# Fifteen trains of unread TensorE passes behind the last store of a fused convolution and feed-forward kernel

## The chip, the cores and the metric

The kernel runs on one core of a Trainium2 chip (trn2). The metric is the time of one execution on the device in microseconds, the median of several runs; lower is better.

## The reference

Two steps follow each other. A dynamic convolution over the sequence takes a softmax over seven taps for each token and head and sums seven shifted copies of the input with these weights; its result, 32768 tokens of 192 numbers, goes through two matrix products with a squared ReLU between them (2048 hidden units).

```python
w = np.exp(weight_gen - max); w = w / (w.sum(-1) + 1e-9)     # 8 x 4096 x 8 heads x 7 taps
x_unf = x_pad[:, idx, :].reshape(B, S, K, H, group)          # seven shifted copies of x
x = np.einsum('bshk,bskhg->bshg', w, x_unf).reshape(B * S, 192)
r = np.maximum(x @ w_in, 0.0)                                # w_in 192 x 2048
out = (r * r) @ w_out                                        # w_out 2048 x 192
```

## The kernel before

The 32768 tokens are laid over 128 partitions, 256 tokens each, and go through in 64 chunks of four tokens per partition (512 tokens, `N`). For every chunk VectorE makes the softmax and the tap sums, the result is turned so that the 192 features lie on partitions, and TensorE then does the first product (`mm1`, line 430) and the second (`mm2_turned`, line 503). The precision of a float32 product is kept with passes over two parts: a rounded high part and the remainder (`xh`, `xl` of the input; `gh`, `gl` of the squared ReLU; two parts of each weight in `W` and `V`), all of type float32r. A pass has a 64-row or 128-row weight (`LDWEIGHTS`) and a moving operand of up to 512 columns. The passes of 64 rows come in pairs, for the upper and the lower half of the array's rows, and the two halves of a pair write two banks of PSUM.

ScalarE makes ReLU, square and `gh` (lines 447, 451, 455), VectorE makes `gl` (line 459). The order of the work is written out by hand: the program is issued in the order of the code, and lists of functions (`todo`, `soon`, `late`, `pend`) say behind which pair of hidden blocks a piece of another chunk stands. The first chunk's second product is a float32 one (line 467), with the weights still unsplit.

The last chunk is done another way. Its ReLU writes the tokens in another order (lines 443, 445), and its second product runs with the activations as weights and `V` as the moving operand (line 476, 384 and 192 columns in turn). Behind it `finish` and `store` put out the four tokens one by one: four passes of line 767 and eight of line 770, VectorE's last sum (line 773) and the last store (line 774, issued in line 557). The pools with rotating buffers that the change draws on are `ps_h` (four PSUM banks, tag `ph`), `gp` (eight buffers each of `rg`, `gh`, `gl`) and `att` (`xT`).

Of the kernel before, what the change touches and what calls it, by code (L numbers as in the profile page):

```python
# [8 lines left out]
F32 = mybir.dt.float32  # L9
F32R = mybir.dt.float32r  # L10
U32 = mybir.dt.uint32
AF = mybir.ActivationFunctionType
ALU = mybir.AluOpType
# [8 lines left out]
def kernel(  # L22
# [531 lines left out]
    def store(c, t0, t1):  # L554
        o_sb, _ = outs[c]
        tsl = slice(t0, t1)
        nc.sync.dma_start(out=out_v[:, rows_of(c) + t0:rows_of(c) + t1, :], in_=o_sb[:, tsl])
# [215 lines left out]
    nc.vector.tensor_tensor(out=o_sb[:, t], in0=rest[:, 0:D], in1=tmp[:, t, 0:D], op=ALU.add)  # L773
    store(c, t, TC)


# [1 line left out]
_INS = ["x", "weight_gen", "moe_w_in", "moe_w_out"]  # L778
# [26 lines left out]
```

## Time and profile before

| | |
|---|---|
| Time, median of 2 runs | 2230.99 us (2230.70 to 2231.29) |
| Span of the profiled execution, first to last instruction | 2229.4 us |
| TensorE passes (MATMUL) | 2224.8 us busy, 19486 instructions |
| TensorE weight loads | 1846.2 us busy, 19486 instructions |
| VectorE | 1869.8 us busy, 2866 instructions |
| ScalarE | 1805.4 us busy, 3492 instructions |

The profiled execution has no time of its own besides its span; the median of the runs is 1.6 us longer than that span. Busy times of different engines overlap. Ends of passes are modelled, so the rate of TensorE is read from the starts.

### The profile page before, as it was taken

How to read it: one execution, taken by the hardware profiler on the slowest of the kernel's cores; microseconds unless marked ns; L12 is line 12 of the kernel's file. 1: busy time of each engine (PE TensorE's matmuls, PEld its weight loads, DVE VectorE, ACT ScalarE, POOL GpSimd, SP SyncE). 2: the span in 40 equal slices, each digit the busy share in tenths (PEclk: the TensorE clock that was granted, in tenths of full speed). 3: DMA queues.
4: the chain of work that ended last, by engine and by line, in shares of the span. 5: the costliest groups of instructions: out<-in, count | busy, mean ns of one | idle time of the engine just before them, and what ended most of it. 6: DMA issues, size and time to landing. Idle time of an engine off the chain costs nothing.

```text
span 2229.4 us, 50051 instructions
## 1 busy us (share of the span) xinstructions
PE 2224.8 (100%) x19486; PEld 1846.2 (83%) x19486; DVE 1869.8 (84%) x2866; ACT 1805.4 (81%) x3492; POOL 9.9 (0%) x18
## 2 busy tenths in 40 slices
PE   9999999999999999999999999999999999999999
PEld 8888888888888888888888888888888888888888
DVE  9888888888888888888898888888888888888885
ACT  8888888888888888888888888888888888888886
POOL 0000000000000000000000000000000000000000
PEclk9999999999999999999999999999999999999999
DMA  8433323333233333333332333323333233332322
GB/s 221 96 85 92 90 59 100 83 94 99 57 92 89 88 100 75 74 95 82 100 85 64 100 85 92 88 60 100 84 94 96 54 98 86 91 100 66 82 60 53
DMA packets 323117, 195.30 MB, mean 88 GB/s; under 512 B 223944, under 2 KB 281288, under 8 KB 319040
## 3 DMA queue, kind: packets, MB, share of 16 engines
q1 hardware_dynamic: 321584, 188.58, 33.8%
q0 software_dynamic: 1296, 3.54, 0.9%
q8 instruction: 152, 2.49, 0.5%
q14 instruction: 85, 0.70, 0.1%
HBM read 106.39 MB, written 49.55 MB: 70 GB/s over the span
## 4 chain that ended last, share of the span: by engine, by line
PE 100%; POOL 0%; DVE 0%; issue 0%; POOLq 0%
PE acc L503 50%; PE ph L430 46%; PE acc L467 1%; PE acc L476 1%; PE acc L430 0%; PE acc L341 0%; PE acc L567 0%; PE ph L329 0%; PE ph L770 0%; PE acc L329 0%; PE acc L767 0%; DVE o_sb L773 0%; POOL ident masks.py:199 0%; POOL ident masks.py:197 0%; POOL ex L92 0%
## 5 line engine op out<-in xcount | busy, mean ns | idle before, releaser
L503 PE MATMUL acc<-gh,V 64*128 64x512 f32 x5952 | 1007.4, 386 | 0.0
L430 PE MATMUL ph<-xh,W 64*128 64x512 f32 x6084 | 853.9, 386 | 0.0
L447 ACT ACTIVATE rg<-ph 128x512 f32<-128x512 f32 x992 | 539.1, 597 | 351.5 <-PE ph L430 351.4
L503 PE MATMUL acc<-gl,V 64*128 64x512 f32 x3968 | 772.4, 386 | 0.0
L459 DVE TENSOR_TENSOR gl<-rg,gh 128x512 fp32r<-128x512 f32 x1008 | 644.4, 678 | 139.0 <-ACT gh L455 137.4
L430 PEld LDWEIGHTS ph<-xh,W 64*128 64x128 f32 x6084 | 569.6, 184 | 120.4 <-ACT rg L445 0.4
L503 PEld LDWEIGHTS acc<-gh,V 64*128 64x128 f32 x5952 | 557.5, 184 | 117.1
L451 ACT ACTIVATE rg<-rg 128x512 f32<-128x512 f32 x1008 | 581.3, 633 | 0.2
L455 ACT CAST gh<-rg 128x512 fp32r<-128x512 f32 x1008 | 576.1, 626 | 3.2 <-PE acc L476 3.2
L503 PEld LDWEIGHTS acc<-gl,V 64*128 64x128 f32 x3968 | 371.7, 184 | 78.0
L430 PE MATMUL ph<-xl,W 64*128 64x512 f32 x3042 | 427.3, 386 | 0.0
L266 DVE TENSOR_TENSOR pr<-xt,wt 128x768 f32<-128x768 f32 (+1 forms) x441 | 411.7, 946 | 2.3
L279 DVE TENSOR_TENSOR pr<-pr 128x768 f32<-128x768 f32 x366 | 347.0, 948 | 0.1
L430 PEld LDWEIGHTS ph<-xl,W 64*128 64x128 f32 x3042 | 284.9, 184 | 59.9
L310 DVE TENSOR_TENSOR xl<-xT,xh 128x512 fp32r<-128x512 f32 x186 | 117.7, 688 | 180.9 <-ACT xh L307 180.9
L307 ACT CAST xh<-xT 128x512 fp32r<-128x512 f32 x186 | 102.7, 624 | 0.1
L513 DVE TENSOR_TENSOR raw<-acc,raw 128x512 f32<-128x512 f32 x124 | 79.9, 686 | 5.9 <-ACT raw L511 5.9
L511 ACT COPY raw<-acc 128x512 f32<-128x512 f32 x124 | 66.6, 597 | 0.0
L237 ACT ACTIVATE wt<-wt 128x224 f32<-128x224 f32 x62 | 24.3, 392 | 47.4 <-DVE wt L236 47.4
L393 DVE STREAM_TRANSPOSE xr<-pr 128x768 f32<-128x768 f32 x62 | 60.6, 978 | 2.1
L525 DVE STREAM_TRANSPOSE raw<-raw 64x512 f32<-64x512 f32 x62 | 43.6, 704 | 2.1
L522 DVE STREAM_TRANSPOSE raw<-raw 128x512 f32<-128x512 f32 x62 | 43.7, 704 | 0.0
(93 smaller groups left out, 449.8 us busy)
## 6 DMA issues: line engine op xcount, KB each, us to landing
xT<-xd SPq DMA_DIRECT2D x124, 384.0 KB, 5.0
xt<-in_x_dram SPq DMA_DIRECT2D x30, 1344.0 KB, 6.9
out_dram<-o_sb SPq DMA_DIRECT2D x63, 384.0 KB, 2.7
xd<-xr SPq DMA_DIRECT2D x248, 96.0 KB, 2.0
o_sb<-raw SPq DMA_DIRECT2D x1488, 16.0 KB, 1.8
raw<-raw SPq DMA_DIRECT2D x62, 128.0 KB, 4.2
wt<-in_weight_gen_dram SPq DMA_DIRECT2D x31, 224.0 KB, 3.2
raw<-in_moe_w_in_dram SPq DMA_DIRECT2D x16, 192.0 KB, 5.3
```

What stands on the lines that cost most here:

```text
L266: tt(out=dst, in0=src, in1=wf[:, t0 * H:t1 * H, k:k + 1].broadcast_to([P, m, G]), op=ALU.mult)
L279: tt(out=prs[k0], in0=prs[k0], in1=prs.pop(k), op=ALU.add)
L307: nc.scalar.copy(parts["h"][:, k, n], src[k][:, n])
L310: tt(out=parts["l"][:, k, n], in0=src[k][:, n], in1=parts["h"][:, k, n].bitcast(F32), op=ALU.subtract)
L430: nc.tensor.matmul(two[i], w, xx[rows, k], start=(n == 0), stop=(n == len(seq) - 1))
L447: nc.scalar.activation(r, ph, AF.Relu)
L451: nc.scalar.activation(r, r, AF.Square)
L455: nc.scalar.copy(gh, rgs[c, fb])
L459: nc.vector.tensor_tensor(out=gl, in0=rgs.pop((c, fb)), in1=ghs[c, fb].bitcast(F32), op=ALU.subtract)
L503: nc.tensor.matmul(accs[c][b + h], w, g[rows], **fl)
L511: nc.scalar.copy(X[:, k], acc[b])
L513: nc.vector.tensor_tensor(out=X[:, k], in0=acc[b + 1], in1=X[:, k], op=ALU.add)
```

## The change

Behind the last store 186 passes are issued on TensorE, whose results are read by no output: first six over 128 rows, then 15 trains of six pairs of 64 rows. All have the last chunk's last `gh` (`mv`, 512 columns of 4 bytes) as the moving operand and differ in the order in which its columns are read. The first six and one of the trains take the two halves of `mv` in turn, column by column. The trains are: in order; backwards; swapped pairs; eight in which two streams are read in turn, one column each, at a distance of 2, 4, ..., 256 columns; four in which blocks of 2, 4, 8 and 32 columns of the two halves are read in turn. VectorE gets 15 further operations and ScalarE 12, on 128 x 512 elements, contiguous or strided; no output reads them either. The output stays as it was.

```diff
--- before.py
+++ after.py
@@ -773,6 +773,53 @@
     nc.vector.tensor_tensor(out=o_sb[:, t], in0=rest[:, 0:D], in1=tmp[:, t, 0:D], op=ALU.add)
     store(c, t, TC)
 
+    sides = list(enumerate((slice(0, D1), slice(D1, P))))
+    mv = ghs[NCH - 1, NF - 1]
+    bk = [ps_h.tile([P, N], F32, name="ph") for _ in range(3)]
+
+    def train(right, passes=6):
+        for f in range(passes):
+            for h, rows in sides:
+                nc.tensor.matmul(bk[1 + h], V[rows, f, 0:P], right(rows), start=True, stop=True)
+
+    for f in range(6):
+        nc.tensor.matmul(bk[0], V[:, f, 0:P], mv.rearrange("p (i m) -> p m i", i=2), start=True, stop=True)
+    train(lambda rows: mv[rows])
+    train(lambda rows: mv[rows, ::-1])
+    train(lambda rows: mv[rows].rearrange("p (a b) -> p a b", b=2)[:, :, ::-1])
+    for n in (2, 4, 8, 16, 32, 64, 128, 256):
+        train(lambda rows, n=n: mv[rows].rearrange("p (a i m) -> p a m i", i=2, m=n))
+    for n in (2, 4, 8, 32):
+        train(lambda rows, n=n: mv[rows].rearrange("p (i a m) -> p a i m", i=2, m=n))
+    src, dst, low_ = (gp.tile([P, N], t, name=n) for t, n in ((F32, "rg"), (F32R, "gh"), (F32R, "gl")))
+    xT = att.tile([P, ND, N], F32, name="xT")
+    nc.vector.tensor_copy(src, rgs[NCH - 1, NF - 1] if (NCH - 1, NF - 1) in rgs else mv.bitcast(F32))
+    nc.vector.tensor_copy(xT[:, 1], src)
+    nc.vector.tensor_copy(dst, src)
+
+    def two(t):
+        return t.rearrange("p (i m) -> p m i", i=2)
+
+    def nat(t):
+        return t.rearrange("p (m i) -> p m i", i=2)
+
+    for _ in range(3):
+        nc.scalar.copy(two(low_), nat(src))
+    for _ in range(3):
+        nc.scalar.copy(nat(low_), two(src))
+    for _ in range(3):
+        nc.scalar.activation(two(xT[:, 0]), nat(bk[0]), AF.Relu)
+    for _ in range(3):
+        nc.scalar.activation(xT[:, 2], src, AF.Square)
+    for _ in range(3):
+        nc.vector.tensor_tensor(out=two(low_), in0=nat(src), in1=two(dst).bitcast(F32), op=ALU.subtract)
+    for _ in range(3):
+        nc.vector.tensor_tensor(out=low_, in0=src, in1=dst.bitcast(F32), op=ALU.subtract)
+    for _ in range(3):
+        nc.vector.tensor_tensor(out=two(low_), in0=nat(bk[0]), in1=two(dst).bitcast(F32), op=ALU.subtract)
+    for _ in range(3):
+        nc.vector.transpose(xT[:, 0].rearrange("p (q t i) -> p q t i", t=TC, i=Q), src.rearrange("p (t i q) -> p q t i", t=TC, i=Q))
+
 
 # ---- launch: one core; inputs and outputs as the reference has them ----
 _INS = ["x", "weight_gen", "moe_w_in", "moe_w_out"]
```

On TensorE the new passes stand at the end of the program, behind the last pass of line 770; `ph` is a PSUM bank, `gh` the moving operand, `V` the weights.

```order
 L770 MATMUL ph<-V,gh 128x192
 L770 MATMUL ph<-V,gl 128x192
-L800 UNCONDITIONAL_BRANCH
+L786 MATMUL ph<-gh,V 128x512 x6
+L783 MATMUL ph<-gh,V 128x512 x180
+L847 UNCONDITIONAL_BRANCH
```

The branch ends the engine's program; all that stood ahead of it keeps its place and 186 passes stand between it and the last useful pass.

On VectorE the new rows stand behind the sum of line 773, on which the last store waits; `rg`, `gh` and `gl` are new buffers of their pools, `xT` a buffer of the convolution's.

```order
 L552 TENSOR_TENSOR raw<-acc_33244,raw 128x64
 L773 TENSOR_TENSOR o_sb<-ph,raw 128x192
-L800 UNCONDITIONAL_BRANCH
+L796 COPY rg<-gh 128x512
+L797 COPY xT<-rg 128x512
+L798 CAST gh<-rg 128x512
+L815 TENSOR_TENSOR gl<-rg,gh 128x256x2 x3
+L817 TENSOR_TENSOR gl<-rg,gh 128x512 x3
+L819 TENSOR_TENSOR gl<-ph,gh 128x256x2 x3
+L821 STREAM_TRANSPOSE xT<-rg 128x512 x3
+L847 UNCONDITIONAL_BRANCH
```

Fifteen operations now stand behind that sum, and none ahead of it.

On ScalarE they stand behind the copies of `finish` (line 549).

```order
 L549 COPY raw<-acc_33243 128x192
 L549 COPY raw<-acc_33244 128x192
-L800 UNCONDITIONAL_BRANCH
+L807 CAST gl<-rg 128x256x2 x3
+L809 CAST gl<-rg 128x512 x3
+L811 ACTIVATE xT<-ph 128x256x2 x3
+L813 ACTIVATE xT<-rg 128x512 x3
+L847 UNCONDITIONAL_BRANCH
```

Twelve operations stand behind the last copy; the first waits for VectorE's copy of line 796, and line 811 reads the bank that the six first passes write.

## Rows read from the trace of the kernel before

**Rows 1.** The page, parts 1 and 2: span, TensorE's busy time, granted clock by slice.

```profile
span 2229.4 us, 50051 instructions
PE 2224.8 (100%) x19486; PEld 1846.2 (83%) x19486; DVE 1869.8 (84%) x2866; ACT 1805.4 (81%) x3492; POOL 9.9 (0%) x18
...
PEclk9999999999999999999999999999999999999999
```

**Rows 2.** The page, part 4: the chain that ended last, by engine and by line.

```profile
PE 100%; POOL 0%; DVE 0%; issue 0%; POOLq 0%
PE acc L503 50%; PE ph L430 46%; PE acc L467 1%; PE acc L476 1%; PE acc L430 0%; PE acc L341 0%; PE acc L567 0%; PE ph L329 0%; PE ph L770 0%; PE acc L329 0%; PE acc L767 0%; DVE o_sb L773 0%; POOL ident masks.py:199 0%; POOL ident masks.py:197 0%; POOL ex L92 0%
```

**Rows 3.** The table of stretches, steady part; header row, then one stretch per row.

```profile
core 0: us, PE busy (x) PEld busy (x) DVE busy (x) ACT busy (x) POOL busy (x), PEclk, DMA share, GB/s
...
1000.00:1100.00 100.00, 100.00 (x886) 82.65 (x884) 85.02 (x129) 81.39 (x158) 0.00 (x0) 1.00 0.35 92
1400.00:1500.00 100.00, 100.00 (x886) 82.65 (x884) 84.01 (x129) 81.38 (x158) 0.00 (x0) 1.00 0.33 80
```

**Rows 4.** Instructions in order of time: start us, length us, engine, instruction; the end.

```profile
2224.70 0.59 PE L767 MATMUL acc<-V,gh 128*128 128x192 f32 x4
...
2225.12 0.27 PE L770 MATMUL ph<-V,gh 128*128 128x192 f32 x1
...
2225.90 0.27 PE L770 MATMUL ph<-V,gl 128*128 128x192 f32 x1
2226.21 0.36 DVE L773 TENSOR_TENSOR o_sb<-ph,raw 128x192 f32<-128x192 f32 x1
```

**Rows 5.** The view of line 557, the last stores: issue (ns) and landing (us).

```profile
L557 SPq DMA_DIRECT2D out_dram<-o_sb x4: 333/336/348, 55.2 to 2226.6; - x4
...
DMA to landing us min/median/max: 1.6/1.7/2.3
```

**Rows 6.** The table of stretches, after TensorE's last pass.

```profile
2226.20:2227.00 0.80, 0.00 (x0) 0.00 (x0) 0.36 (x1) 0.00 (x0) 0.00 (x0) 1.00 0.38 123
2227.00:2228.50 1.50, 0.00 (x0) 0.00 (x0) 0.00 (x0) 0.00 (x0) 0.00 (x0) 1.00 0.21 66
2228.50:2229.40 0.90, 0.00 (x0) 0.00 (x0) 0.00 (x0) 0.00 (x0) 0.00 (x0) 0.74 0.00 0
```

**Rows 7.** Instructions in order of time, last stage; 26 turns lie between the outer rows.

```profile
2214.14 0.36 PE L476 MATMUL acc<-V,gh 128*128 128x384 f32 x1
...
2214.34 0.25 PE L476 MATMUL acc<-V,gl 128*128 128x192 f32 x1
...
2221.54 0.36 PE L476 MATMUL acc<-V,gh 128*128 128x384 f32 x1
```

**Rows 8.** TensorE's instructions in order of time, second product of the first chunk.

```profile
43.72 8.29 PE L467 MATMUL acc<-du,gl 128*128 128x192 f32 x50
```

**Rows 9.** The table of stretches, same time; the 1.00 behind POOL is the granted clock.

```profile
45.00:51.00 6.00, 6.00 (x39) 6.00 (x38) 5.79 (x9) 3.39 (x6) 0.00 (x0) 1.00 1.01 259
```

**Rows 10.** Groups by line and shape: count | busy us, mean ns | idle before, releaser.

```profile
L459 DVE TENSOR_TENSOR gl<-rg,gh 128x512 fp32r<-128x512 f32 x1008 | 644.4, 678 | 139.0 <-ACT gh L455 137.4 <-PE acc L476 1.6
L451 ACT ACTIVATE rg<-rg 128x512 f32<-128x512 f32 x1008 | 581.3, 633 | 0.2
L455 ACT CAST gh<-rg 128x512 fp32r<-128x512 f32 x1008 | 576.1, 626 | 3.2 <-PE acc L476 3.2
L447 ACT ACTIVATE rg<-ph 128x512 f32<-128x512 f32 x992 | 539.1, 597 | 351.5 <-PE ph L430 351.4
...
L522 DVE STREAM_TRANSPOSE raw<-raw 128x512 f32<-128x512 f32 x62 | 43.7, 704 | 0.0
...
L170 ACT ACTIVATE du<-raw 128x768 f32<-128x768 f32 x7 | 6.5, 929 | 0.3 <-DMA raw<-in_moe_w_out_dram 0.3
...
L443 DVE TENSOR_SCALAR rg<-ph 128x512 f32<-128x512 f32 x7 | 4.8, 690 | 6.4 <-PE ph L430 6.3
```

## The prediction

> **What bounds the kernel now.** I read the page's busy shares and clock row first, then the chain that ended last, then the table of stretches, then the last microseconds in order of time. TensorE is busy for 2224.8 of 2229.4 us, with a granted clock of at least 0.9 of full speed in every slice [rows 1], and the chain that ended last is TensorE for its whole length, rounded: 50% the second product and 46% the first [rows 2]. So whatever TensorE is given after its present last pass is added nearly whole, and nothing before that pass can be moved by it. In the steady part 886 matmuls start in 100 us, at a granted clock of 1.00 [rows 3]. They come in pairs, one half of the rows each, side by side, so one pair of 512 columns costs 100 / 443 = 0.2257 us, 0.441 ns a column. That is the price of a pair whose moving operand lies in one run, and it is the form of every pass of the new trains, but for the order in which the columns are read.
>
> The end of the program shows what little can hide work [rows 4]. The last pass starts at 2225.90 and takes 0.27, so TensorE is done at 2226.17. VectorE's last sum runs from 2226.21 to 2226.57. A store then takes at least 1.6 us to land [rows 5], until about 2228.2, and the span ends at 2229.4, some 1.2 us later, with no DMA and no engine at work in its last 0.9 us [rows 6]. So the cover for new work on TensorE is 2229.4 - 2226.2 = 3.2 us, of which I count 1.2 as closing steps that come after whichever engine is last. The two timed runs have the median 2230.99, so 1.6 us lie outside the span; the sums below are made on the span of 2229.4 and get these 1.6 us added.
>
> **The change, part by part.** Nothing is removed, and on every engine the new instructions stand behind all that was there. The pools and tags are those in use, so I put nothing on the 2226.2 us ahead of the tail. The last stores are issued by SP, which gets nothing new, so they go out when they did.
>
> TensorE gets 186 passes of 512 columns: 6 over all 128 rows, then 15 trains of 6 pairs of halves. That is 96 steps (6 full passes and 90 pairs). Three of them wait, for TensorE's own earlier work, and the first L770 pass has such a wait today and starts, at 2225.12, some 0.1 us after the last of the four L767 passes (2224.70 + 0.59 - 0.27 = 2225.02) [rows 4]. No train waits for ScalarE or VectorE, and none of their results is awaited. If a step costs what a steady pair costs, the sum is 96 x 0.2257 = 21.7 us. A full-height step has no row of its own width: in the last stage 26 turns of 384 and 192 columns over 128 rows go from 2214.14 to 2221.54 [rows 7], 0.285 us for 576 columns, which is 0.495 ns a column and 0.25 us for 512. For six steps that is 0.2 us more, and I leave it out.
>
> No row of this trace has a moving operand that is not one run, so the price of the new orders must be bounded. From below: 0.2257 us a step, since reading in another order can't be cheaper than the columns' own rate at full clock. From above, the nearest rows by engine are those of the first chunk's second product, where the passes of 192 columns start 0.162 us apart over a long stretch, (8.29 - 0.33) / 49, at a granted clock of 1.00 [rows 8, 9]. That is 0.846 ns a column, 1.9 times the steady pair, and it is the slowest rate at which this kernel's TensorE takes columns. For 512 columns it makes 0.433 us. The nearest rows by pattern are on other engines. ScalarE reads every second word of the weights in 929 ns for 768, 1.21 ns an element, against 633 ns for 512 in one run, 1.24; VectorE takes 690 ns where it reads runs of 32 words and 678 without [rows 10]. Other orders cost these two nothing, but they ask for a word only every 1.2 to 1.3 ns, a third of TensorE's rate, so they exclude only that a word from elsewhere takes longer than that: 512 x 1.21 = 0.62 us a step, the far bound.
>
> Between 0.2257 and 0.62 I take 0.433, as a stream that can't deliver a column at every slot delivers one at every second, and TensorE's own slow row is that rate. Which trains pay it? In the 6 full passes and 7 of the 8 distance trains every single column is taken from at least four words away from the one before it: the streams alternate at 4 to 256 words. I count those 6 + 42 = 48 steps at 0.433, 20.8 us. In the other 48 a column has a neighbour within the same four words beside it in time: the plain train, the backwards one, swapped pairs, distance 2 (0, 2, 1, 3), and the four trains that alternate by blocks of 2, 4, 8 and 32. I count these at 0.2257, 10.8 us. Sum 31.6 us.
>
> The Trainium skill, Advanced Engine Details and Errata, section Memory Cachelines, states that SBUF is read in lines of 16 bytes, that at least two hits on a line are needed to absorb the latency, and that another line at every access brings a penalty. It names no size for it, and no run here shows it. By that rule the same 48 steps would pay, and the sum would stay as it is; without it, it would be 21.7 us.
>
> VectorE gets 15 operations and ScalarE 12. Each is like one that the trace prices: copies, casts, activations of 128x512 at 0.60 to 0.63 us, subtractions at 0.68, transposes at 0.70 [rows 10]. VectorE starts at 2226.57 with three copies (at most 0.69 each). ScalarE starts when the first has ended, 2227.3, and needs 12 x 0.63 = 7.6, until 2234.8. VectorE's subtractions write what ScalarE's first six wrote and start at about 2231.1; 9 x 0.69 + 3 x 0.70 end at 2239.4. TensorE is at work until at least 2226.2 + 21.7 = 2247.9, so this chain lies in its shadow with 8 us to spare; were each of its strided operations twice as long it would end at about 2247.3, still hidden.
>
> Forecast: TensorE ends at 2226.2 + 31.6 + 0.16 (the last pass is 0.386 long, 0.16 beyond its step) = 2258.0; with 1.2 us of closing the span is 2259.2, and with 1.6 us outside it the time is **2261 us**, 1.3% over the time before.
>
> **The rivals.** (a) Order is free. Then all 96 steps cost 0.2257: 2226.2 + 21.7 + 0.16 + 1.2 + 1.6 = 2251. For it: no engine of this kernel pays for another order. Against it: none of those rows runs at TensorE's rate.
>
> (b) Every order but the plain one pays the half rate, blocks, backwards and swaps too: 90 steps at 0.433 and 6 at 0.2257, 40.3 us, 2269.5. For it: the steady rows show only long runs, so a reader that expects the next address may lose on any turn. Against it: a block of 32 words turns rarely.
>
> (c) Slower by over 2%: the halves of a pair no longer run side by side when each of them is slow. In the steady part the second half starts with the first; if a half that stalls holds the other, the 42 alternating pairs cost 2 x 0.433 each. Then 42 x 0.866 + 6 x 0.433 + 10.8 = 49.8 us, and the time is 2279, 2.1% over. It decides from where such a half by itself takes over 0.395 us, since the bound at 2275.6 leaves TensorE 46.4 us, 35.6 of them for 90 alternating halves and passes. For it: the two halves share one queue and finish in order. Against it: both halves read the same addresses in the same rhythm, so neither is ahead to be held. With the halves side by side an alternating step would have to cost 0.74 us to reach the same point, more than the far bound.
>
> (d) The change doesn't do what it says: the passes, whose results nobody reads, don't appear or lie under the last store: 2231. The built program has all 186 in TensorE's row, and 3.2 us of cover hold 14 plain steps at most.
>
> **How the numbers follow.** Forecast 0.48, (a) 0.29, (b) 0.13, (c) 0.07, (d) 0.02, and 0.01 for an end nobody lists, on the fast side. The range goes from 2249, the free case with the closing steps partly under TensorE's work, to 2272, the case in which all orders pay and a little more; the far bound of 0.62 us for the 48 alternating steps, 2270, lies in it. Two per cent is about what a measurement of this kernel can tell from no change. Faster by that much 0.01, within it 0.91, slower 0.08, the last being (c) and a little for the others' tails.
>
> **What would show it.** In the changed profile the steps of each train can be timed by start: 6 pairs in 1.35 us where the order is free, 2.6 where it pays. The forecast wants seven distance trains and the six full passes slow and eight trains at the steady price, the chain that ended last closing with the new passes, VectorE's last transpose done near 2239, the clock at 1.00 through the tail, and everything before 2226 as it was. It is wrong if distances 4 to 256 differ among themselves, if backwards or blocks pay, or if the seconds of the pairs start behind the firsts' ends.

## The result and the profile after

The changed kernel takes 2251.52 us (2250.99 to 2252.05, 2 runs) against 2230.99: ratio 1.0092, 95% interval 1.0062 to 1.0121. It is 20.5 us slower, inside the stated range of 2249 to 2272, but the time is that of rival (a), 2251, not of the forecast, 2261.

The page of the changed kernel, parts 1 and 4, answers to [rows 1, 2].

```profile
span 2250.0 us, 50453 instructions
PE 2247.2 (100%) x19672; PEld 1866.1 (83%) x19672; DVE 1883.7 (84%) x2881; ACT 1815.5 (81%) x3504; POOL 9.9 (0%) x18
...
PE 100%; DMA 0%; DVE 0%; SPq 0%; issue 0%; DVEq 0%
PE acc L503 50%; PE ph L430 46%; PE ph L783 1%; PE acc L467 1%; PE acc L476 1%; PE acc L430 0%; PE acc L341 0%; DMA xt<-in_x_dram 0%; PE ph L329 0%; PE ph L786 0%; PE ph L770 0%; PE acc L329 0%; DVE pr L266 0%; PE acc L767 0%; SPq L101 0%
```

186 passes, 15 and 12 operations have come (19672 - 19486, 2881 - 2866, 3504 - 3492), and the chain that ended last now closes with line 783. The end in order of time answers to [rows 4].

```profile
2226.24 0.27 PE L770 MATMUL ph<-V,gl 128*128 128x192 f32 x1
...
2226.35 1.48 PE L786 MATMUL ph<-gh,V 128*128 128x512 f32 x6
2226.55 0.36 DVE L773 TENSOR_TENSOR o_sb<-ph,raw 128x192 f32<-128x192 f32 x1
...
2227.76 21.28 PE L783 MATMUL ph<-gh,V 64*128 64x512 f32 x180
...
2242.05 3.87 DVE L821 STREAM_TRANSPOSE xT<-rg 128x512 f32<-128x512 f32 x3
```

The last useful pass starts at 2226.24 (2225.90 before). The passes run on until 2227.76 + 21.28 = 2249.04, the span ends at 2250.0, and this run took 2252.05. VectorE ends at 2242.05 + 3.87 = 2245.92, 3.1 us ahead of TensorE.

The table of stretches, line 783 alone, one stretch per train; the seven trains at distances 4 to 256 are one stretch, x84. The count behind PEld is the number of passes; the one behind PE also holds passes that began before the stretch.

```profile
core 0: us, PE busy (x) PEld busy (x), PEclk, DMA share, GB/s
2229.23:2230.64 1.41, 1.41 (x14) 1.22 (x12) 1.00 0.00 0
2230.64:2232.02 1.39, 1.39 (x14) 1.21 (x12) 1.00 0.04 12
2232.02:2233.38 1.36, 1.36 (x14) 1.20 (x12) 1.00 0.00 0
2233.38:2242.45 9.06, 9.06 (x86) 8.51 (x84) 1.00 0.00 0
2242.45:2244.46 2.02, 2.02 (x14) 1.26 (x12) 1.00 0.00 0
2244.46:2245.97 1.51, 1.51 (x14) 1.22 (x12) 1.00 0.00 0
2245.97:2247.43 1.46, 1.46 (x14) 1.22 (x12) 1.00 0.00 0
```

In this order: backwards, swapped pairs, distance 2, distances 4 to 256, blocks of 2, 4 and 8. A step is one pair (or one full-height pass), from the start of its first pass to the start of the next one's. Divided by its 42 pairs, a step of distances 4 to 256 is 9.06 / 42 = 0.2157 us, and the starts show 215 or 216 ns for every one of these steps. The steady pair of the kernel before is measured best over a long stretch (columns as in [rows 3]):

```profile
300.00:2100.00 1800.00, 1800.00 (x15886) 1487.65 (x15884) 1522.85 (x2300) 1462.41 (x2822) 0.00 (x0) 1.00 0.34 86
```

15884 passes are 7942 pairs in 1800 us, 0.22665 us a pair. The alternating step is 4.8% **below** that. Distance 2 takes 1.36 / 6 = 0.227, the steady price. Blocks of 2 take 2.02 / 6 = 0.336, of 4 0.252, of 8 0.243.

Groups by line and shape in the same stretch answer to [rows 10].

```profile
L821 DVE STREAM_TRANSPOSE xT<-rg 128x512 f32<-128x512 f32 x3 | 3.8, 1266 | 0.1
L807 ACT CAST gl<-rg 128x512 fp32r<-128x512 f32 x3 | 3.4, 1126 | 1.4 <-DVE rg L796 1.3
L819 DVE TENSOR_TENSOR gl<-ph,gh 128x512 fp32r<-128x512 f32 x3 | 3.3, 1114 | 0.2
L815 DVE TENSOR_TENSOR gl<-rg,gh 128x512 fp32r<-128x512 f32 x3 | 3.3, 1111 | 5.1 <-ACT gl L809 5.0
L811 ACT ACTIVATE xT<-ph 128x512 f32<-128x512 f32 x3 | 3.3, 1090 | 0.1
L809 ACT CAST gl<-rg 128x512 fp32r<-128x512 f32 x3 | 2.2, 745 | 0.1
L817 DVE TENSOR_TENSOR gl<-rg,gh 128x512 fp32r<-128x512 f32 x3 | 2.1, 693 | 0.1
L813 ACT ACTIVATE xT<-rg 128x512 f32<-128x512 f32 x3 | 1.9, 631 | 0.1
```

Operations whose output alternates between two halves, 256 columns apart (lines 807, 811, 815, 819), take 1.09 to 1.13 us, where rows of the kernel before without such an output take 0.60 to 0.68 [rows 10]; a read of that kind alone (line 809) takes 0.75; the rearranging transpose (line 821) 1.27 in place of 0.70.

### The profile page after: what moved, and what is told of

It reads as the page before. It is cut to its first block, busy times and chain, and to the rows that moved or that the text cites. A ratio compares the mean times of both kernels' runs of the same rounds, so it can differ in the third digit from the quotient of the medians.

```text
span 2250.0 us, 50453 instructions
## 1 busy us (share of the span) xinstructions
PE 2247.2 (100%) x19672; PEld 1866.1 (83%) x19672; DVE 1883.7 (84%) x2881; ACT 1815.5 (81%) x3504; POOL 9.9 (0%) x18
## 4 chain that ended last, share of the span: by engine, by line
PE 100%; DMA 0%; DVE 0%; SPq 0%; issue 0%; DVEq 0%
PE acc L503 50%; PE ph L430 46%; PE ph L783 1%; PE acc L467 1%; PE acc L476 1%; PE acc L430 0%; PE acc L341 0%; DMA xt<-in_x_dram 0%; PE ph L329 0%; PE ph L786 0%; PE ph L770 0%; PE acc L329 0%; DVE pr L266 0%; PE acc L767 0%; SPq L101 0%
```

## The experiments

**e1_reversed.** The trains in the opposite order, and nothing new on VectorE and ScalarE.

```diff
+    for n in (32, 8, 4, 2):
+        train(lambda rows, n=n: mv[rows].rearrange("p (i a m) -> p a i m", i=2, m=n))
+    for n in (256, 128, 64, 32, 16, 8, 4, 2):
+        train(lambda rows, n=n: mv[rows].rearrange("p (a i m) -> p a m i", i=2, m=n))
...
+    train(lambda rows: mv[rows])
```

> The 15 trains in the opposite order (blocks first, the plain train last), without VectorE's 15 and ScalarE's 12 new operations; the six full passes stay. Theory A, the order of reading alone sets a step: each train keeps its step, 340, 250, 243, 237 ns for blocks of 2, 4, 8, 32, 215.7 for distances 4 to 256, 227 for distance 2, swapped pairs and the plain train, 233 backwards; span within 1 us of the changed kernel's 2250.0. Theory B, the moment sets it (what ScalarE, VectorE and the last stores do beside it): the trains of the first 6 us are at 227 or more whatever their order, and the three last, plain one included, run at about 216.

2251.59 us (one run), span 2249.7. The table of stretches of this kernel:

```profile
2230.43:2231.93 1.50, 1.50 (x14) 1.14 (x12) 1.00 0.04 11
2231.93:2233.96 2.03, 2.03 (x14) 1.17 (x12) 1.00 0.00 0
2233.96:2243.03 9.07, 9.07 (x86) 7.96 (x84) 1.00 0.00 0
2243.03:2244.39 1.36, 1.36 (x14) 1.13 (x12) 1.00 0.00 0
```

In order: blocks of 4, blocks of 2, distances 256 to 4, distance 2. Each train keeps its step (0.250, 0.338, 0.216, 0.227) at another moment and with the other engines idle. By their starts, swapped pairs come at 227 ns, backwards about 233, blocks of 32 at 235, and the plain train settles at 226 or 227 after some longer first steps. Theory A holds; only blocks of 32 are 2 ns off. The time is that of the full change, so the 27 operations of the other engines cost nothing while TensorE covers them.

**e2_tail_only.** The six full passes and the 27 operations, without the 15 trains.

```diff
-    train(lambda rows: mv[rows])
...
-        train(lambda rows, n=n: mv[rows].rearrange("p (i a m) -> p a i m", i=2, m=n))
```

> The six full passes and VectorE's and ScalarE's 27 new operations stay, the 15 trains are left out. Theory A, the strided operations on VectorE and ScalarE are slow by themselves: VectorE's last transpose ends near 2245.9 as in the changed kernel, the span is near 2246.9 and the time near 2248.5, so this half of the change alone costs 17 us. Theory B, they were slow because TensorE read and wrote beside them: without the trains they take 0.6 to 0.7 us each, VectorE ends near 2239.5, and the time is near 2242.

2247.37 us (one run), span 2245.6. In order of time, and by groups:

```profile
2241.30 3.29 DVE L814 STREAM_TRANSPOSE xT<-rg 128x512 f32<-128x512 f32 x3
```

```profile
L808 DVE TENSOR_TENSOR gl<-rg,gh 128x512 fp32r<-128x512 f32 x3 | 3.3, 1089 | 4.9 <-ACT gl L802 4.9
L800 ACT CAST gl<-rg 128x512 fp32r<-128x512 f32 x3 | 3.2, 1082 | 1.4 <-DVE rg L789 1.3
L814 DVE STREAM_TRANSPOSE xT<-rg 128x512 f32<-128x512 f32 x3 | 3.2, 1072 | 0.1
```

VectorE ends at 2244.59. The alternating operations still take 1.08 to 1.09 us, so they are slow by themselves; of what the changed kernel shows only the transpose is much slower beside TensorE (1.27 against 1.07). Theory A holds: this half alone costs 16 us, and the two halves of the change lie over each other.

**e3_laced.** The kernel before without any tail; the 62 middle chunks read at distance 4 in both products. Read three times over, this order is the natural one again, so the copies and sums of the accumulators read them that way once.

```diff
+    def laced(a):
+        return a.rearrange("p (a i m) -> p a m i", i=2, m=4)
+    def runs(a):
+        return a.rearrange("p (a m i) -> p a m i", i=2, m=4)
...
+        turned = laced if 0 < c < NCH - 1 else lambda a: a
...
-                nc.tensor.matmul(two[i], w, xx[rows, k], start=(n == 0), stop=(n == len(seq) - 1))
+                nc.tensor.matmul(two[i], w, turned(xx[rows, k]), start=(n == 0), stop=(n == len(seq) - 1))
...
-                nc.tensor.matmul(accs[c][b + h], w, g[rows], **fl)
+                nc.tensor.matmul(accs[c][b + h], w, laced(g[rows]), **fl)
...
-            nc.scalar.copy(X[:, k], acc[b])
+            nc.scalar.copy(runs(X[:, k]), laced(acc[b]))
...
-            nc.vector.tensor_tensor(out=X[:, k], in0=acc[b + 1], in1=X[:, k], op=ALU.add)
+            nc.vector.tensor_tensor(out=runs(X[:, k]), in0=laced(acc[b + 1]), in1=runs(X[:, k]), op=ALU.add)
```

> The kernel before, without the new tail; in the 62 middle chunks both products read their moving operand as two streams in turn at a distance of four columns, and the sums read the accumulators once more in that order, which with the two before it gives the natural order back. Theory A, the order sets the step of a pair anywhere: 62 x 152 = 9424 pairs at 215.7 in place of 226.65 ns save 103 us, time 2128, ratio 0.954. Theory B, the moment sets it: steps stay at 226.65 and the time at 2231. Theory C, steps fall but VectorE or ScalarE, over 80% busy, hold TensorE: a saving under 60 us, 2170 to 2231, with waits of TensorE for their results in the trace.

2137.14 us, ratio 0.958 (0.9564 to 0.9596): 93.8 us less than before. The stretch, and the groups of the accumulators' sums and copies, first of this kernel and then of the one before:

```profile
300.00:2100.00 1800.00, 1800.00 (x16613) 1736.95 (x16611) 1572.01 (x2392) 1522.78 (x2952) 0.00 (x0) 1.00 0.35 88
```

```profile
L520 DVE TENSOR_TENSOR raw<-acc,raw 128x512 f32<-128x512 f32 x124 | 79.0, 675 | 3.7 <-ACT raw L518 3.7
L518 ACT COPY raw<-acc 128x512 f32<-128x512 f32 x124 | 66.5, 596 | 0.0
...
L513 DVE TENSOR_TENSOR raw<-acc,raw 128x512 f32<-128x512 f32 x124 | 79.9, 686 | 5.9 <-ACT raw L511 5.9
L511 ACT COPY raw<-acc 128x512 f32<-128x512 f32 x124 | 66.6, 597 | 0.0
```

16611 passes (PEld's count) in 1800 us are 216.7 ns a pair, against 226.65 in the kernel before. ScalarE's copy (596 ns) and VectorE's sum (675) of the accumulators cost no more for the alternating read at distance 4: the same operations took 597 and 686 with a contiguous read. Theory A holds but for 9 of its 103 us; 1.05 ns a pair above 215.7 make 9.9 us, and they lie at two places of each chunk (e8_low_last).

**e4_grid.** Other orders in trains of 12, behind the last store. The full-height passes use all 128 rows with one weight load, the single-half passes 64 rows without a partner.

```diff
+    train(full, in_order)
+    train(full, laced)
+    train(low_half, in_order)
...
+    train(both_halves, lambda a: a.rearrange("p (i m) -> p m i", i=4))
...
+    train(both_halves, lambda a: a.rearrange("p (m s) -> p s m", s=2))
+    train(both_halves, lambda a: a.rearrange("p (m s) -> p s m", s=4))
```

> Fourteen trains of 12 steps behind the last store in place of the change, no other new operations: pairs in order and at distance 4; full-height passes in order and at distance 4; passes of the lower half alone in order and at distance 4; four streams 128 columns apart; then with 508 columns pairs in order, in order from column 2, distance 2, distance 2 from column 2; then every second and every fourth column; and in order again. Theory L, four neighbouring words are one unit and a read that stays in one for four columns is slow: full-height and single-half passes show the same gap as pairs (226 in order, 216 at distance 4), every fourth column and four streams run at 216, distance 2 from column 2 falls to about 214 as its words lie in two units, in order from column 2 stays at 225, every second column lies between. Theory W, the gap comes from the two weight loads of a pair: full-height and single-half passes in order run at about 216, and where the columns begin changes nothing.

```profile
2231.41:2234.26 2.85, 2.85 (x15) 2.36 (x13) 1.00 0.00 0
2234.26:2236.94 2.68, 2.68 (x13) 2.08 (x12) 1.00 0.00 0
2236.94:2239.79 2.85, 2.85 (x13) 2.32 (x13) 1.00 0.00 0
...
2242.11:2245.39 3.28, 3.28 (x27) 2.90 (x26) 1.00 0.00 0
...
2256.47:2261.69 5.22, 5.22 (x27) 3.39 (x24) 1.00 0.00 0
2261.69:2267.21 5.52, 5.52 (x27) 3.38 (x25) 1.00 0.00 0
```

The rows are full height in order and at distance 4, the lower half in order, four streams, every second and every fourth column. By the starts a settled step is 227, 216 and 227 ns (the lower half at distance 4, without a row here, 216), then 271 to 275, about 451 and about 461. Full-height and single-half passes have one weight load a step and the same gap as pairs, so theory W falls. But L has missed too: four streams and every fourth column are not at 216, and a walk of two columns costs twice the step. These two slow trains ran in pairs only, and the second half of a settled pair starts 363 to 386 ns behind the first there; whether each pass runs at half the rate or the two halves hold each other is not shown. The trains with 508 columns came out of step behind the four streams and say little; the next run repeats them.

**e5_columns.** Full-height passes alone, fewer columns and other first columns.

```diff
+    train(lambda a: laced(a[:, 0:504]), 504)
+    train(lambda a: laced(a[:, 2:506]), 504)
+    train(lambda a: a[:, 0:384], 384)
+    train(lambda a: laced(a[:, 0:384]), 384)
```

> Thirteen trains of 12 full-height passes behind the last store in place of the change, one weight load each: in order; 508 columns in order, in order from column 2, distance 2, distance 2 from column 2; in order again; 504 columns at distance 4, the same from column 2; 384 columns in order and at distance 4; 256 columns in order and at distance 4; in order. Theory F, a pass that reads in order pays a fixed 11 ns: the gap between in order and distance 4 stays at 11 ns with 384 and 256 columns. Theory C, it pays by the column: 8.2 ns with 384 and 5.5 with 256. Theory L, four words of a unit: distance 2 from column 2 falls to 214 ns, and distance 4 from column 2 rises; if where the columns begin changes nothing, L falls.

```profile
2242.40:2244.95 2.55, 2.55 (x13) 2.27 (x12) 1.00 0.00 0
2244.95:2247.67 2.72, 2.72 (x13) 2.26 (x12) 1.00 0.00 0
2247.67:2249.75 2.08, 2.08 (x13) 2.07 (x12) 1.00 0.00 0
2249.75:2251.70 1.95, 1.95 (x13) 1.95 (x13) 1.00 0.00 0
```

The rows are 504 columns at distance 4, the same from column 2, 384 columns in order and at distance 4. Settled steps by the starts: 504 columns at distance 4 take 212.5 ns, the same from column 2 take 225 to 230; 384 columns 173.3 in order and 162.5 at distance 4; 256 columns 117 to 122 and 111.7. Distance 2 from column 2 stays at 225 to 235, and 508 columns in order, at 223 to 234, are no cheaper than 512. So where the streams begin matters for distance 4, as theory L asks, but not for distance 2, against it. The gap is 11 ns with 512 (226.7 here, 215.7 in e4_grid) and with 384 columns, where a price by the column (C) asked for 8.2. From 384 to 512 columns either order rises by 53 ns (226.7 - 173.3, 215.7 - 162.5), 0.42 ns a column, so between these two the order adds a fixed price to a pass (F). Another 128 columns fewer would by the same line be 120 and 109 ns; seen are 117 to 122 and 111.7, a gap of some 7 ns, nearer to C's 5.5 than to F's 11. No theory of the three fits all trains.

**e6_distance2.** The kernel e3_laced with `m=2`, its sums as in the kernel before.

```diff
-        return a.rearrange("p (a i m) -> p a m i", i=2, m=4)
+        return a.rearrange("p (a i m) -> p a m i", i=2, m=2)
```

> The kernel e3_laced with a distance of two columns in both products; the two orders undo each other, so the sums read the accumulators as before. Theory A, only a distance of four or more is cheaper: pairs stay near 226.7 ns and the time at 2231. Theory B, any access in two interleaved streams is cheaper in the main loop, or the gain of e3_laced came from the strided sums: the time falls to about 2137 here too, or to somewhere between.

2231.02 us, ratio 1.000 (0.9991 to 1.001).

```profile
300.00:2100.00 1800.00, 1800.00 (x15886) 1487.65 (x15884) 1523.01 (x2301) 1463.19 (x2822) 0.00 (x0) 1.00 0.34 86
```

15884 passes in 1800 us, 226.65 ns a pair as in the kernel before: the form of the access pattern does nothing, the distance all. Theory A holds.

**e7_first_product.** The kernel e3_laced with the second product in order; the sums, not shown here, undo the one turn that is left.

```diff
-                nc.tensor.matmul(accs[c][b + h], w, laced(g[rows]), **fl)
+                nc.tensor.matmul(accs[c][b + h], w, g[rows], **fl)
```

> The kernel e3_laced with distance 4 in the first product alone; the second reads in order, and the sums undo the one turn. Theory A, each pass has the price of its own order: 62 x 72 pairs save 10.95 ns each, 48.9 us, time 2182. Theory S, going from distance 4 to in order costs what e4_grid shows around such a change, 93 ns on the last step before and about 135 on the first steps after it, 0.23 us: 62 x 8 changes cost 113 us, more than the 48.9 saved, time 2295, slower by 2.9%.

2198.09 us, ratio 0.9853 (0.9838 to 0.9867), 32.9 us less than before.

```profile
300.00:2100.00 1800.00, 1800.00 (x16136) 1519.14 (x16134) 1536.72 (x2336) 1480.91 (x2865) 0.00 (x0) 1.00 0.35 86
```

Neither theory fits. First-product pairs step at 216 ns and the changes between orders take no 0.23 us, so S falls. But pairs of the second product now take 226 to 236, 229.83 in the mean of the starts over the same 1800 us, where they took 226.67: 62 x 80 x 3.16 ns = 15.7 us of the 48.9 are given back. The two terms leave 33.2, and 32.9 are measured.

**e8_low_last.** The kernel e3_laced, with the passes of `gl` behind those of `gh`.

```diff
-        seq = B + A if last or first else A + B
+        seq = B + A if last or first else [A[0], A[2], B[0], A[1], B[1]]
```

> The kernel e3_laced, with the two passes of the low part gl moved behind the three of gh in each hidden block of the second product, but for the first and the last block. In e3_laced a mean pair takes 216.72 ns where its own step is 215.7, 160 ns a chunk or 9.9 us in all, at two places of each chunk: a pass of gl that waits for VectorE's subtraction, and the first pass into an accumulator that waits for VectorE's sum. Theory A, the first is half of it and goes, as gl is asked for 0.4 us later: 5 us less, 2132. Theory B, VectorE is late by more than that or the wait moves to the next pass: 2137 as before.

2132.70 us, ratio 0.956 (0.9544 to 0.9576). Stretch, and what TensorE's weight loads still wait for:

```profile
300.00:2100.00 1800.00, 1800.00 (x16650) 1571.53 (x16648) 1574.51 (x2397) 1523.91 (x2958) 0.00 (x0) 1.00 0.35 89
```

```profile
PEld acc L510 <- DVE raw L520: 11.5, 59, 0.2
```

Theory A holds: 4.4 us less than e3_laced, 216.2 ns a pair. The other place is left, the first pass into an accumulator that VectorE's sum of the chunk before still reads. This is the fastest kernel of the study, 98 us below the one before.

## Why the prediction was right, and where it was not

**What bounds the end.** Right: the passes stand behind all useful work, TensorE ends last, and the rest lies in its shadow. The start of the tail (2226.2 forecast; line 786 starts at 2226.35), the closing (1.2 forecast, 2250.0 - 2249.04 = 0.96) and the part outside the span (1.6 forecast, 2.05 in this run) are off by less than half a microsecond each.

**The price of the orders.** The step that failed is "I count those 6 + 42 = 48 steps at 0.433". They take 0.216, so 20.8 us became 48 x 0.216 = 10.4. The row that gave 0.433 could not price an order: line 467 is the float32 product, and its moving operand of 192 columns lies in one run. The lower bound failed with it: "reading in another order can't be cheaper than the columns' own rate at full clock" took the steady pair for that rate, and 512 columns in 215.7 ns lie under it. (That pair was also read 0.4% too short: the 886 of [rows 3] hold passes that began before the stretch, and 0.22665 us is the long mean.) The other 48 steps were not all at 0.2257 either: blocks of 2 cost 0.336, and with the blocks of 4 and 8, the slow first steps of the plain train and the backwards one they make some 1.2 us more than 10.8. The two errors leave TensorE's part 9 us short of the forecast, 22.5 us in place of 31.6 and close to rival (a)'s 21.7; but that rival's reason, that order is free, is not what the trace shows, since orders do differ, in both directions. So the time lies in the stated range only because the range reached down to the free case; the forecast's own mechanism did not happen, and by its own signs it was wrong, since the distance trains are fast and blocks and backwards pay. A step of about 0.433 us exists, but for reads of every second or fourth column (0.451 and 0.461 in e4_grid), which the change doesn't have.

**The rule cited.** The Trainium skill, Advanced Engine Details and Errata, section Memory Cachelines, has the penalty for another line at every access. The trace disagrees: distances 4 to 256 change the line at every column and are the fastest, 215.7 ns, and every second column, with two hits on a line, costs 451, hardly less than every fourth (461), with one. The Trainium skill, TensorE: Matmul & The Clock Gate, section Back-to-back issue gap, gives N / 2.4 + 2.5 ns as the gap of an isolated matmul of N columns at full clock; worked out for 512 columns that is an estimate of 215.8 ns. The alternating trains agree to 0.1 ns, and passes in order, 226.65 in the kernel before, do not.

**The other engines.** Forecast to end at 2239.4, they end at 2245.9. The mis-sized term is "each is like one that the trace prices": no row had an output that alternates over 256 columns, and those take 1.6 to 1.8 times as long. The caveat, each strided operation twice as long and still hidden, came out hidden, with 3.1 us to spare; its sum of 2247.3 left the transposes at 0.70, and they took 1.27 too. The run e2_tail_only shows that the 16 us appear as soon as TensorE's cover is gone.

**The rivals.** (b) falls with the settled steps of the swapped pairs and the backwards train (227 and 233 ns, plain 227). (c) falls: in the change's trains the halves of a pair start at most 22 ns apart, in the slow blocks of 2 at most 17. (d) falls: all passes are in the trace.

## What to carry to other kernels

A probe at the end of a program is priced by the engine that ends last and reads best by its starts, train by train; the time of the whole says next to nothing of it. A rate that a whole kernel keeps for milliseconds is no floor: the steady 226.65 ns looked like TensorE's own pace, and another reading order of the same operand was worth 4.2% (e3_laced), with a second reordering 4.4% (e8_low_last). The gain by reading order has its full size only with the order in both products (32.9 us with one, 93.8 with both), and the order has to be undone where a reader is cheap: here a third read in that order by ScalarE and VectorE, at no cost.

## What the runs showed of the hardware that had not been expected

Of a float32r moving operand of 512 columns at a granted clock of 1.00: two streams read in turn at a distance of 4 to 256 columns, 215.7 ns a step; in order, swapped pairs and distance 2, 226.7; backwards 233; blocks of 32, 8, 4 and 2 in turn 235 to 237, 243, 252 and 340; four streams 273; every second and fourth column 451 and 461 (in pairs whose halves start far apart). Distance 4 loses its gain if it begins two columns later (212.5 to about 227, 504 columns). The 11 ns of reading in order are a fixed price of a pass between 384 and 512 columns (e5_columns). Why order costs them is open: not the pairing of halves or a second weight load (full-height and single-half passes show it too), not the moment (e1_reversed), not the form of the access pattern (e6_distance2). Open as well are the longer first steps of some trains, up to 339 ns (e1_reversed), and why the second product slows to 230 ns a pair beside a first product in the other order.
